# Linear attention into an MLP: k and q loaded ahead of v, and the output step of two head pairs done at once

## The chip, the cores and the metric

The kernel runs on one core of one Trainium2 chip. Its time is the device time of one execution in microseconds (us); the times quoted are medians of several executions. Lower is better. A core has TensorE (PE in the profile, with its weight loads as PEld), VectorE (DVE), ScalarE (ACT), GpSimd (POOL) and SyncE (SP), which work side by side, each through its own instructions in order, and wait for each other on semaphores.

## The reference

Attention with a decay, in blocks of 64 positions, for 4 batches, 8 heads, 768 positions and 64 columns a head; then an MLP with 512 inputs, 2048 hidden columns and 512 outputs over all 3072 tokens.

```python
for b in range(nb):                                   # blocks of 64 positions, in order
    qb, kb, vb = q[:, :, sl], k[:, :, sl], v[:, :, sl]
    intra = einsum('bhic,bhjc->bhij', qb, kb) * Dmask     # lam ** (i - j) for i >= j, else 0
    intra = einsum('bhij,bhjd->bhid', intra, vb)
    inter = einsum('bhid,bhde->bhie', qb * lam_pow, kv_state)
    out[:, :, sl] = intra + inter
    kv_state = lam_block * kv_state + einsum('bhsd,bhse->bhde', kb * rev_pow, vb)
x = out.transpose(0, 2, 1, 3).reshape(B * S, H * D)
h = x @ w_in
return (h / (1 + exp(-1.702 * h))) @ w_out
```

The kernel's own block is 128 positions long; the result is the same.

## The kernel before

**Waves.** The 3072 tokens are done in six waves of 512. Waves 2 to 5 each take 128 positions of all four batches. Waves 0 and 1, on which the change bears, take the first 256 positions of two batches each (`load_big`, `big_cast`, `big_t`, `big_s`, `big_m`, `big_kv`, `big_c`, `big_st`). The eight heads are four pairs, p = 0 to 3; one pair fills the 128 partitions.

**One pair of waves 0 and 1** goes through these steps:

- `load_big` loads k, q or v of some heads, as two DMAs, one for each batch (L96).
- `big_cast` multiplies k and q by powers of lam and casts them to bf16 (L225), on DVE (`V`) or GpSimd (`G_`); `big_cast_v` casts v on GpSimd (L229).
- `big_t` transposes k and q on PE (L238) and copies them out of PSUM, k on ACT (L242), q on ACT or DVE (L240).
- `big_s` makes the scores (L255) and `big_m` masks them on DVE (L262) into `sm` buffers, of which the pool holds six (L261); a pair takes two.
- `big_kv` makes the state of two pairs (L279), in two PSUM banks, one for each half of the 256 positions. ACT copies the first half's state into `mid`, which the second half's output needs (L283, two copies, one for each head), and once more into `first` (L284).
- `big_st` combines the two halves' states on DVE for wave 2 (L291), reading the second half from PSUM.
- `big_c` makes the output of one pair: two full-array matmuls with `mid` (L299) and sixteen on quarter arrays with v and the masked scores (L307), into two banks, which one engine (ACT; DVE for pair 3) casts to `xT` (L311), the MLP's input.

**PSUM.** `bank` hands out eight banks in two rings: three with the tag `mm` (MLP, some transposes) and five with the tag `att`. A step that takes the next bank of its ring waits until its last reader is done.

**MLP.** `mlp1` makes a hidden column block (fc, sixteen of them) from four input blocks kc = 0 to 3, one for each pair (L378), and ACT applies the gelu (L381); `mlp2` makes an output of 128 tokens in four items j (L391). In waves 0 and 1 the first three column blocks (`EARLY = 3`) are started in parts, as the pairs come in: [0, 1], then [2], then [3].

**Order.** The kernel writes each engine's order out by hand (`manual_schedule`); nothing is moved later. The head, wave 0's attention, stands in the main body as a list of calls. Then `main` lists the MLP items wave by wave, and `side` holds calls with the index of the main item ahead of which they are made. `BIG` is that list for wave 1's attention, which so lies among wave 0's `mlp2` items. Matmuls called `fill` multiply zeros while PE has nothing to do.

**Loads.** SP's queue takes the loads of wave 0 in the order q and k of pairs 0 and 1, then v of heads 0 to 3, k, q and v of heads 4 to 7; one DMA that waits for the second block of w_out (`sync_behind_weights`, L188); then wave 1 in the order k, q, v of heads 0 to 3 and k, q, v of heads 4 to 7; then wave 2. Weights come through GpSimd's queue (L176, L180), between its casts. Waves 2 to 5 are cast by `do_cast` and transposed by DMAs on SP's queue (L205).

Of the kernel before, what the change touches and what calls it, by code (L numbers as in the profile page):

```python
# [24 lines left out]
def kernel(  # L25
# [78 lines left out]
    def begin():  # L104
# [8 lines left out]
        for nm, h0 in (("v", 0), ("k", 4), ("q", 4), ("v", 4)):  # L113
            load_big(0, nm, h0, 4, nc.sync)
# [50 lines left out]
    first_sb = [const.tile([P, 2, BB, D], bf16, name=f"first{i}") for i in range(2)]  # L165
# [25 lines left out]
    cast, trans, masked, xT, g_of, h_ps, o_ps, vbig, sc_of, kv_of = ({} for _ in range(10))  # L191
# [27 lines left out]
    def big_cast(w, nm, p, eng):  # L219
# [4 lines left out]
        for bb in range(BB):  # L224
            eng.tensor_tensor(x[:, bb].rearrange("p t (h d) -> p h t d", h=2), pair_of(w, nm, p)[:, bb], by, op=MUL)  # L225
# [6 lines left out]
    def big_t(w, p, q_out=None, mm=None):  # L232
        kq = work.tile([P, 2, BB, 2, P], bf16, tag=f"kq{p}", name="kqB")
        for i, nm in enumerate("kq"):
# [4 lines left out]
            if nm == "q" and q_out is not None:  # L239
                q_out.tensor_copy(kq[:, i], ps_t)  # L240
            else:
                nc.scalar.copy(kq[:, i], ps_t)  # L242
        trans[w, p] = kq
# [24 lines left out]
    def big_kv(w, p0, mm, fills=0):  # L268
# [12 lines left out]
        for h in range(2):  # L281
            hs = slice(64 * h, 64 * h + 64)
            nc.scalar.copy(mid_sb[p0 // 2][hs, :, :, hs], ps_kv[0][hs])  # L283
        nc.scalar.copy(first_sb[p0 // 2], ps_kv[0])  # L284
        kv_of[w, p0] = ps_kv[1]

    def big_st(w, p0):
        ps_kv = kv_of.pop((w, p0))
# [5 lines left out]
    def big_c(w, p, fills=0, x_out=None):  # L294
        vb, qT = vbig[w, p], trans[w, p][:, 1]
        ps_o = [bank([P, BB, 2, D], f32, f"ps_o{r}") for r in range(2)]
        fill(ps_o[0].rearrange("p b t s -> p (b t s)"), fills)
        for bb in range(BB):
            nc.tensor.matmul(ps_o[1][:, bb], mid_sb[p // 2][:, p % 2, bb, :], qT[:, bb, :, D:P],  # L299
                             start=(bb == 0), stop=False, skip_group_check=True)  # L300
        for bb in range(BB):
            for t in range(2):
# [239 lines left out]
```

## Time and profile before

| | us |
|---|---|
| median of three executions | 215.24 |
| lowest, highest | 214.95, 216.2 |
| profiled execution | 215.14 |
| its span, first to last instruction | 213.4 |
| PE busy | 204.8 |
| ACT, DVE, POOL busy | 87.4, 83.8, 33.2 |

The page's second part cuts the span into 40 slices, one digit each, the busy share in tenths. The groups give line, engine, operation, shapes and count, then the busy time in us, the mean length in ns, the idle time ahead of them and what ended it. A line of the timeline has start and busy time in us, then the same names, and in brackets the idle time ahead and its releaser. A busy time of PE includes about 0.2 us in which the last matmul runs out, while the next may have begun.

### The profile page before, as it was taken

To read this page: it belongs to the slowest core of one execution; us is meant where nothing else is said; L and a number is where in the kernel's file an instruction comes from. 1 tells how busy PE (TensorE), PEld (TensorE's weight loads), DVE (VectorE), ACT (ScalarE), POOL (GpSimd) and SP (SyncE) were. 2 spreads that over 40 slices of the span, in tenths; PEclk is the share of its full clock that TensorE was granted. 3 is DMA by queue.
4 is the path that set the end of the run, shared out by engine and by line. 5 is a ranking of instruction groups with operands and counts; after the bars stand their busy time and mean duration, and the time that the engine had idled before them with its cause. 6 is when DMAs were issued, how large, how long until landed. Compare 5 with 4: busy or idle time off the path is not lost.

```text
span 213.4 us, 4323 instructions
## 1 busy us (share of the span) xinstructions
PE 204.8 (96%) x1757; PEld 101.1 (47%) x1757; DVE 83.8 (39%) x186; ACT 87.4 (41%) x164; POOL 33.2 (16%) x62
## 2 busy tenths in 40 slices
PE   7779999999999999999999999999999999999994
PEld 2454444545444455444545444545444545444453
DVE  3687100285751573624272624272624071100121
ACT  4683673445666122366302366302376302466000
POOL 4599000562130012101110001120000000000000
PEclk9999999999999999999999999999999999999999
DMA  5999999999899989699981399981390012100112
GB/s 137 268 248 198 203 197 248 295 267 200 186 276 213 198 190 229 221 188 223 221 195 52 114 184 223 227 191 56 114 178 0 3 51 94 53 2 0 49 49 98
DMA packets 88839, 33.83 MB, mean 159 GB/s; under 512 B 68724, under 2 KB 85876, under 8 KB 88820
## 3 DMA queue, kind: packets, MB, share of 16 engines
q1 hardware_dynamic: 83524, 29.11, 57.9%
q0 software_dynamic: 4752, 4.19, 12.5%
q10 hardware_dynamic: 544, 0.26, 0.5%
q8 instruction: 13, 0.21, 0.4%
q14 instruction: 6, 0.05, 0.1%
HBM read 27.27 MB, written 6.29 MB: 157 GB/s over the span
## 4 chain that ended last, share of the span: by engine, by line
PE 91%; DMA 4%; DVE 1%; ACT 1%; POOL 1%; SPq 0%; issue 0%; POOLq 0%
PE ps_h L378 39%; PE ps_out L391 38%; DMA vb<-in_v_dram 2%; PE ps_o L362 2%; PE ps_o L355 2%; PE ps_s L321 2%; PE ps_part L402 2%; DMA qb<-in_q_dram 2%; PE ps_o L307 1%; PE ps_s L255 1%; PE ps_kv L279 1%; PE ps_kv L338 1%; ACT xT L311 1%; PE ps_tq L238 1%; ACT g_sb L381 1%; POOL vb L229 1%
## 5 line engine op out<-in xcount | busy, mean ns | idle before, releaser
L378 PE MATMUL ps_h<-xT,w_in 128*128 128x512 bf16 x384 | 85.3, 379 | 1.1 <-ACT xT L311 0.5
L391 PE MATMUL ps_out<-w_out,g_sb 128*128 128x512 bf16 x368 | 83.7, 379 | 0.0
L381 ACT ACTIVATE g_sb<-ps_h 128x512 bf16<-128x512 f32 x96 | 56.9, 597 | 44.9 <-PE ps_h L378 44.6
L378 PEld LDWEIGHTS <-w_in 128*128 128x128 bf16 x384 | 37.0, 98 | 45.5 <-issue 1.6
L391 PEld LDWEIGHTS <-g_sb 128*128 128x128 bf16 x368 | 34.5, 98 | 40.2
L325 DVE SCALAR_TENSOR_TENSOR sm<-ps_s,inv_pow,mask 128x512 bf16<-128x512 f32 x32 | 21.8, 744 | 28.6 <-PE ps_s L321 28.6
L395 DVE COPY o_sb<-ps_out 128x512 f32<-128x512 f32 x19 | 13.1, 691 | 47.0 <-PE ps_out L391 46.6
L367 ACT CAST xT<-ps_o 128x512 bf16<-128x512 f32 x16 | 8.6, 589 | 44.4 <-PE ps_o L362 44.4
L202 POOL CAST v_sb<-vf 128x512 bf16<-128x512 f32 x16 | 10.4, 652 | 84.8 <-DMA vf<-in_v_dram 84.8
L225 DVE TENSOR_TENSOR kqb<-kb,kb_pow 128x256 bf16<-128x256 f32 x14 | 6.3, 492 | 19.7 <-DMA kb<-in_k_dram 17.1
L262 DVE SCALAR_TENSOR_TENSOR smb<-ps_s,inv_pow,mask_b 128x512 bf16<-128x512 f32 x16 | 11.0, 745 | 5.9 <-PE ps_s L255 4.8
L345 DVE SCALAR_TENSOR_TENSOR kv<-kv,blk_pow,ps_kv 128x256 bf16<-128x256 bf16 x12 | 5.2, 478 | 17.2 <-PE ps_kv L338 17.2
L200 DVE TENSOR_SCALAR kqs<-qf,q_pow 128x256 bf16<-128x256 f32 x32 | 11.1, 348 | 0.6 <-DMA qf<-in_q_dram 0.6
L225 POOL TENSOR_TENSOR kqb<-qb,qb_pow 128x256 bf16<-128x256 f32 x12 | 7.8, 663 | 22.0 <-DMA qb<-in_q_dram 19.7
L199 DVE TENSOR_SCALAR kqs<-kf,k_pow 128x256 bf16<-128x256 f32 x32 | 11.1, 347 | 0.0
L395 ACT COPY o_sb<-ps_out 128x512 f32<-128x512 f32 x4 | 2.3, 585 | 10.4 <-PE ps_out L391 10.4
L242 ACT COPY kqB<-ps_tk 128x512 bf16<-128x512 bf16 x8 | 4.6, 594 | 2.5 <-PE ps_tk L238 2.4
L238 PEld LDWEIGHTS <-kqb 128*128 128x128 bf16 x64 | 3.9, 98 | 3.6 <-DVE kqb L225 1.3
L355 PEld LDWEIGHTS <-kv 64*64 64x64 bf16 x128 | 3.8, 106 | 3.4 <-issue 3.4
L217 PE MATMUL fill<-warm 128*128 128x512 bf16 x10 | 4.0, 584 | 1.3 <-DVE i_blk L135 1.3
L321 PEld LDWEIGHTS <-kqT 64*128 64x128 bf16 x128 | 3.6, 94 | 3.4 <-issue 3.4
L229 POOL CAST vb<-vb 128x512 bf16<-128x512 f32 x8 | 4.7, 616 | 3.3 <-DMA vb<-in_v_dram 3.2
(61 smaller groups left out, 99.5 us busy)
## 6 DMA issues: line engine op xcount, KB each, us to landing
out_dram<-o_sb SPq DMA_DIRECT2D x23, 256.0 KB, 2.0
kf<-in_k_dram SPq DMA_DIRECT2D x32, 128.0 KB, 3.3
qf<-in_q_dram SPq DMA_DIRECT2D x32, 128.0 KB, 3.5
vf<-in_v_dram SPq DMA_DIRECT2D x32, 128.0 KB, 3.4
vb<-in_v_dram SPq DMA_DIRECT2D x8, 256.0 KB, 5.2
w_out<-in_moe_w_out_dram POOLq DMA_DIRECT2D x4, 512.0 KB, 14.2
kb<-in_k_dram SPq DMA_DIRECT2D x6, 256.0 KB, 5.5
qb<-in_q_dram SPq DMA_DIRECT2D x6, 256.0 KB, 5.9
```

Source lines behind the costliest of these rows:

```text
L199: nc.vector.tensor_scalar(ks[:, :, h, :], kf[:, :, h, :], scalar1=k_pow[:, hd : hd + 1], scalar2=None, op0=MUL)
L200: nc.vector.tensor_scalar(qs[:, :, h, :], qf[:, :, h, :], scalar1=q_pow[:, hd : hd + 1], scalar2=None, op0=MUL)
L202: nc.gpsimd.tensor_copy(v_sb[w % 2][p], vf)
L225: eng.tensor_tensor(x[:, bb].rearrange("p t (h d) -> p h t d", h=2), pair_of(w, nm, p)[:, bb], by, op=MUL)
L262: nc.vector.scalar_tensor_tensor(sm.rearrange("p b t s -> p b (t s)"), s2.rearrange("p b t s -> p b (t s)"), inv_pow[:, 2 * p + h : 2 * p ...
L325: nc.vector.scalar_tensor_tensor(sm, s2[p, h], inv_pow[:, 2 * p + h : 2 * p + h + 1], mask.to_broadcast([P, B, P]), op0=MUL, op1=MUL)
L355: nc.tensor.matmul(ps_o[p][hs, b, :], kv_sb[w % 2][p][hs, b, :], trans[w, p][hs, 1, b, :], start=(b == 0), stop=False, skip_group_check=True)
L367: nc.scalar.copy(x, ps_o[p].rearrange("p b s -> p (b s)"))
L378: nc.tensor.matmul(h_ps[fc], w_in_sb[j][:, kc, i * P : (i + 1) * P], xT[w, kc], start=(kc == 0), stop=(kc == KC - 1))
L381: nc.scalar.activation(g_of[w][:, fc, :], h_ps.pop(fc), GELU)
L391: nc.tensor.matmul(ps_out, g_of[w][:, fc, g * P : (g + 1) * P], w_out_sb[j][:, fc % CW, :], start=(fc == 0), stop=(fc == FFC - 1))
L395: (nc.scalar.copy if w == 0 else nc.vector.tensor_copy)(o, ps_out)
```

## The change

- Loads: in wave 0 v of heads 0 to 3 goes behind k and q of heads 4 to 7; in wave 1 all k and q go ahead of all v.
- Order of the head: transposes and scores of all four pairs are made before the states; then state of pairs 0 and 1, output of pairs 0 and 1, state of pairs 2 and 3, output of pairs 2 and 3; then the MLP, whose early parts are now [0, 1] and [2, 3]. In `BIG` wave 1 is ordered in the same way.
- `big_c` does two pairs in one call: four mid matmuls, thirty-two quarter ones, two banks that each hold both pairs; ACT casts one bank, DVE the other. `xT` is one tile for two pairs (`x_tile`), in all waves.
- `big_kv` copies both halves' states to SBUF as f32 (`part_sb`, on ACT), where `first_sb` held one in bf16; for pairs 2 and 3 one of the two mid copies is on DVE. `big_st` combines the states on GpSimd, two operations a pair, where DVE did one.
- Some casts change engine, the fills are set anew, and some weight loads are called later.

```diff
-        for nm, h0 in (("v", 0), ("k", 4), ("q", 4), ("v", 4)):
+        for nm, h0 in (("k", 4), ("q", 4), ("v", 0), ("v", 4)):
...
-        for h in range(2):
+        for h, eng in enumerate(engs):
             hs = slice(64 * h, 64 * h + 64)
-            nc.scalar.copy(mid_sb[p0 // 2][hs, :, :, hs], ps_kv[0][hs])
-        nc.scalar.copy(first_sb[p0 // 2], ps_kv[0])
-        kv_of[w, p0] = ps_kv[1]
+            eng(mid_sb[p0 // 2][hs, :, :, hs], ps_kv[0][hs])
+        for r in range(2):
+            nc.scalar.copy(part_sb[p0 // 2][r], ps_kv[r])
...
     def big_st(w, p0):
-            nc.vector.scalar_tensor_tensor(kv_sb[0][p][:, BB * w : BB * w + BB], first_sb[p0 // 2][:, i],
-                                           blk_pow[:, p : p + 1], ps_kv[:, i], op0=MUL, op1=ADD)
+            nc.gpsimd.tensor_scalar(part_sb[p0 // 2][0][:, i], part_sb[p0 // 2][0][:, i], scalar1=blk_pow[:, p : p + 1],
+                                    scalar2=None, op0=MUL)
+            nc.gpsimd.tensor_tensor(kv_sb[0][p][:, BB * w : BB * w + BB], part_sb[p0 // 2][0][:, i],
+                                    part_sb[p0 // 2][1][:, i], op=ADD)
...
+    def big_c(w, p0, fills=0):
+        ps_o = [bank([P, 2, BB, 2, D], f32, f"ps_o{r}") for r in range(2)]
...
+        x = x_tile(w, p0)
+        for r, eng in enumerate((nc.scalar.copy, nc.vector.tensor_copy)):
+            eng(x.rearrange("p i (b r s t) -> p r (i b) t s", b=BB, r=2, t=2)[:, r],
+                ps_o[r].rearrange("p i b t s -> p (i b) t s"))
+
+    def x_tile(w, p0):
+        x = xp.tile([P, 2, W], bf16, tag=f"x{p0}", name="xT")
+        for i in range(2):
+            xT[w, p0 + i] = x[:, i]
+        return x
...
-    BIG = [(27, big_cast, "k", 0, V), (27, big_cast, "q", 0, G_), (27, big_cast, "k", 1, V), (27, big_cast, "q", 1, G_),
-           (27, big_cast_v, 0), (27, big_cast_v, 1), (30, big_t, 0), (31, big_t, 1), (31, big_s, 0), (31, big_m, 0),
-           (32, big_s, 1), (32, big_m, 1), (32, big_cast, "k", 3, G_), (32, big_cast, "k", 2, V),
-           (34, big_kv, 0, False), (34, big_cast, "q", 2, G_), (34, big_cast, "q", 3, V), (34, big_st, 0),
-           (35, big_c, 0), (35, big_c, 1), (35.5, big_t, 2, V, True), (36, big_t, 3, V),
-           (36.5, big_s, 2), (36.5, big_m, 2), (37, big_s, 3), (37, big_m, 3), (37, big_cast_v, 2), (37, big_cast_v, 3),
-           (38, big_kv, 2, False), (41, big_c, 2), (41, big_c, 3, 0, V.tensor_copy), (41, big_st, 2)]
+    AV = (nc.scalar.copy, V.tensor_copy)
+    BIG = [(24, big_cast, "k", 0, V), (24, big_cast, "q", 0, G_), (24, big_cast, "k", 1, V), (24, big_cast, "q", 1, G_),
+           (24, big_cast, "k", 2, G_), (27, big_t, 0), (28, big_t, 1), (28, big_s, 0), (28, big_m, 0),
+           (29, big_cast, "k", 3, V), (29, big_s, 1), (29, big_m, 1),
+           (29, big_cast, "q", 2, G_), (29, big_cast, "q", 3, V),
+           (31, big_t, 2, "kq", AV, True), (31, big_t, 3, "kq", AV), (31, big_cast_v, 0), (31, big_cast_v, 1),
+           (32, big_s, 2), (32, big_m, 2), (32, big_s, 3), (32, big_m, 3),
+           (33, big_kv, 0, False), (33, big_cast_v, 2), (33, big_cast_v, 3), (34, big_c, 0), (34, big_kv, 2, False, 0, AV),
+           (35, big_c, 2), (36, big_st, 0), (36, big_st, 2)]
...
-        return ([(mlp1, w, fc, kcs) for kcs in ([0, 1], [2], [3]) for fc in range(EARLY)]
+        return ([(mlp1, w, fc, kcs) for kcs in ([0, 1], [2, 3]) for fc in range(EARLY)]
...
+        big_cast(0, "k", 2, G_)
+        load_w_in(0)
+        load_w_in(1)
+        f1 = bank([P, W], f32, "fill", True)
+        fill(f1, 6)
+        big_cast(0, "k", 3, V)
+        big_cast(0, "q", 2, V)
+        big_cast(0, "q", 3, V)
+        big_t(0, 2, "k")
+        big_t(0, 3, "k")
+        big_t(0, 2, "q")
+        big_t(0, 3, "q")
         big_cast_v(0, 0)
         big_cast_v(0, 1)
...
+        big_s(0, 2)
+        big_m(0, 2)
+        big_s(0, 3)
+        big_m(0, 3)
+        big_kv(0, 0, True)
+        big_c(0, 0, 2)
...
+        big_kv(0, 2, False, 2, AV)
+        big_c(0, 2)
         late_mask()
+        big_st(0, 0)
+        big_st(0, 2)
         sync_behind_weights()
         big_tiles(1)
-        for g in range(2):
-            for nm in "kqv":
-                load_big(1, nm, 4 * g, 4, nc.sync)
+        for nm, h0 in (("k", 0), ("q", 0), ("k", 4), ("q", 4), ("v", 0), ("v", 4)):
+            load_big(1, nm, h0, 4, nc.sync)
```

Because the early items are six where they were nine, an index in the new `BIG` stands for the same place as one three higher in the old.

More of the change, by code (lines that the diff above doesn't have):

```diff
@@ L164 @@
     kv_sb = [[const.tile([P, B, D], bf16, name=f"kv{i}{p}") for p in range(NP)] for i in range(2)]
-    first_sb = [const.tile([P, 2, BB, D], bf16, name=f"first{i}") for i in range(2)]
+    part_sb = [[const.tile([P, 2, BB, D], f32, name=f"part{i}{r}") for r in range(2)] for i in range(2)]
     mid_sb = [const.tile([P, 2, BB, P], bf16, name=f"mid{i}") for i in range(2)]
@@ L364, in mix @@
         ps_kv = state_mm(w, pairs)
-        for p in pairs:
-            x = xp.tile([P, W], bf16, tag=f"x{p}", name="xT")
-            nc.scalar.copy(x, ps_o[p].rearrange("p b s -> p (b s)"))
-            xT[w, p] = x
+        x = x_tile(w, pairs[0])
+        for i, p in enumerate(pairs):
+            nc.scalar.copy(x[:, i], ps_o[p].rearrange("p b s -> p (b s)"))
         state_up(w, pairs, ps_kv)
```

83 lines of the change are left out of this document (30 added, 53 removed).

## The prediction

> **What bounds the kernel now.** I read the page first: its busy times, its slices, and the groups that give the prices of single operations (the last row is of the groups of PE in the first 60 us).
>
> ```profile
> PE 204.8 (96%) x1757; PEld 101.1 (47%) x1757; DVE 83.8 (39%) x186; ACT 87.4 (41%) x164; POOL 33.2 (16%) x62
> PE   7779999999999999999999999999999999999994
> PEclk9999999999999999999999999999999999999999
> L395 DVE COPY o_sb<-ps_out 128x512 f32<-128x512 f32 x19 | 13.1, 691 | 47.0 <-PE ps_out L391 46.6
> L367 ACT CAST xT<-ps_o 128x512 bf16<-128x512 f32 x16 | 8.6, 589 | 44.4 <-PE ps_o L362 44.4
> L262 DVE SCALAR_TENSOR_TENSOR smb<-ps_s,inv_pow,mask_b 128x512 bf16<-128x512 f32 x16 | 11.0, 745 | 5.9 <-PE ps_s L255 4.8
> L299 PE MATMUL ps_o<-kqB,mid 128*128 128x128 bf16 x16 | 2.3, 223 | 0.0
> ```
>
> PE is the bound: only the first slices (5.3 us each) are not full. So the change can act in two places: before the MLP of wave 0 has its inputs, and where wave 1's attention is woven into wave 0's output matmuls. Behind that all code is the same but for the layout of xT. Next, PE in order of time (start, busy, what, idle before).
>
> ```profile
> 20.96 1.46 PE L378 MATMUL ps_h<-xT,w_in 128*128 128x512 bf16 x6 [0.27 <-ACT xT L311]
> 22.67 11.38 PE L378 MATMUL ps_h<-xT,w_in 128*128 128x512 bf16 x52 [0.25 <-ACT g_sb L381]
> 33.90 7.07 PE L391 MATMUL ps_out<-w_out,g_sb 128*128 128x512 bf16 x32
> 40.80 0.39 PE L238 MATMUL ps_tk<-ident,kqb 128*128 128x128 bf16 x4
> ...
> 46.20 0.45 PE L279 MATMUL ps_kv<-vb,kqb 64*64 64x64 bf16 x32
> 46.58 1.04 PE L391 MATMUL ps_out<-w_out,g_sb 128*128 128x512 bf16 x4
> 47.60 0.29 PE L299 MATMUL ps_o<-kqB,mid 128*128 128x128 bf16 x2
> ...
> 48.17 0.28 PE L299 MATMUL ps_o<-kqB,mid 128*128 128x128 bf16 x2
> 48.38 0.42 PE L307 MATMUL ps_o<-smb,vb 64*64 64x128 bf16 x16
> 48.73 1.04 PE L391 MATMUL ps_out<-w_out,g_sb 128*128 128x512 bf16 x4
> ...
> 55.45 0.42 PE L307 MATMUL ps_o<-smb,vb 64*64 64x128 bf16 x16
> 56.15 1.46 PE L378 MATMUL ps_h<-xT,w_in 128*128 128x512 bf16 x6 [0.27 <-ACT xT L311]
> 57.85 10.52 PE L378 MATMUL ps_h<-xT,w_in 128*128 128x512 bf16 x48 [0.25 <-ACT g_sb L381]
> ```
>
> From 22.67 to 33.90 are 52 matmuls, 0.216 us each. Twelve of the 64 ran before, so wave 0's MLP stands as if it had begun at 22.67 - 12 x 0.216 = 20.08 without a gap. That is the head's figure to beat. In wave 1 time is lost in three places: 47.60 - (46.58 + 4 x 0.216) = 0.16 for the mid copies, (56.15 - 55.45) - (48.73 - 48.38) = 0.35 for xT, and 57.85 - (56.15 + 6 x 0.216) = 0.41 for the first gelu.
>
> **The head, part by part.** When loads land is read where an idle engine was released by them. These are POOL, DVE, ACT in their order of time.
>
> ```profile
> 10.34 1.17 POOL L229 CAST vb<-vb 128x512 bf16<-128x512 f32 x2 [2.10 <-DMA vb<-in_v_dram]
> 13.96 0.61 POOL L225 TENSOR_TENSOR kqb<-qb,qb_pow 128x256 bf16<-128x256 f32 x1 [0.19 <-DMA qb<-in_q_dram]
> 16.05 1.18 POOL L229 CAST vb<-vb 128x512 bf16<-128x512 f32 x2
> 12.17 1.10 DVE L225 TENSOR_TENSOR kqb<-kb,kb_pow 128x256 bf16<-128x256 f32 x3 [0.39 <-DMA kb<-in_k_dram]
> 13.19 1.67 DVE L225 TENSOR_TENSOR kqb<-qb,qb_pow 128x256 bf16<-128x256 f32 x2
> 20.73 0.78 DVE L311 CAST xT<-ps_o 128x256 bf16<-128x256 f32 x2 [1.03 <-PE ps_o L307]
> 11.91 0.76 ACT L283 CAST mid<-ps_kv 64x256 bf16<-64x256 f32 x2
> ```
>
> *Loads.* The four-head transfers end at about 10.3 (v 0), 12.2 (k 4) and 13.9 (q 4); v 4 follows one step later, about 15.7. Same bytes, same queue, so the slots stay and the contents change: k 4 at 10.3, q 4 at 12.2, v 0 at 13.9, v 4 at 15.7. GpSimd takes the cast of k of pair 2 when it lands, then issues two weight loads, then the casts of v: k's two casts stand where v's two stood, so the weights come about when they did.
>
> *k, q, scores.* DVE's casts for pairs 2 and 3 (six left to it, at a step of about 0.34 from the 12.17 row) run from 11.3 to 13.4; transposes, copies and all scores are done before 15. They are hidden behind v: v 0's casts take 13.9 to 15.1 (1.17), and now they are done at 11.5. This is the price of the reordering.
>
> *The serial tail.* State matmuls of pairs 0 and 1 end at 15.5 (half of 0.45 behind the last cast); two ACT mid copies 0.76, so 16.3; the double output step for pairs 0 and 1 from 16.35. It costs 0.85: two single steps now take 48.73 - 47.60 = 1.13. In one of them 48.38 - 48.17 = 0.21 pass from the first mid matmul to the first quarter-array one, where two mid matmuls need a step of 0.07 each (0.29 busy, 0.22 for one); the 0.14 left is a switch of the array, and joining drops two. The last mask of pair 3 now waits: `sm` has six buffers (L261), pairs 0 to 2 hold all six, and the first is freed when the double step has read pair 0: 0.35 to its first quarter matmul, 0.2 for sixteen, 0.22 for the last to end, so at 17.1. In the order before, pair 0's output step had long run by then. So on DVE: two masks, 0.66 apart, start 17.1, DVE free at 18.45; then its half of xT; then its half of the second mid copy. A DVE cast of 128x512 from PSUM has no row; it lies between 0.69 (the f32 copy, L395) and 0.78 (two casts of 128x256); I take 0.69, as size and source are the same, of which 0.60 before the next may start. The mid half lies between 0.37 (ACT's 0.76 for two) and 0.44 (half of 0.78 and the overlap); I take 0.44, DVE's own. That gives 19.1 and 19.5. The second double step starts at 19.55, and the MLP, 0.9 with the switch, at 20.45. Behind it nothing waits: its xT needs 0.69 and the six matmuls ahead of [2, 3] give 1.29; the first gelu, 0.6, lies under the rest. 20.45 against 20.08: **+0.37**. The copies of both states into f32 and GpSimd's combination run beside it; were they not hidden, ACT's two copies would add about 0.6.
>
> **Wave 1.** DVE, POOL and SP there:
>
> ```profile
> 43.17 2.73 DVE L262 SCALAR_TENSOR_TENSOR smb<-ps_s,inv_pow,mask_b 128x512 bf16<-128x512 f32 x4 [3.34 <-PE ps_s L255]
> 40.51 1.75 POOL L225 TENSOR_TENSOR kqb<-qb,qb_pow 128x256 bf16<-128x256 f32 x3 [0.21 <-DMA qb<-in_q_dram]
> 45.92 0.78 POOL L225 TENSOR_TENSOR kqb<-qb,qb_pow 128x256 bf16<-128x256 f32 x1 [0.28 <-DMA qb<-in_q_dram]
> 47.83 1.17 POOL L229 CAST vb<-vb 128x512 bf16<-128x512 f32 x2 [1.13 <-DMA vb<-in_v_dram]
> 62.73 6.21 SPq L205 DMA_TRANSPOSE kqT<-kqs  x4
> ```
>
> Here too the slots stay: v 0 takes the slot that ended at 45.9, v 4 that of 47.8. All PE times shift by the 0.37.
>
> - *q of pair 3.* DVE now does masks of pair 0 (from 43.54, two steps of 0.66), k of pair 3 (0.68), masks of pair 1 (1.32): q of pair 3 starts at 46.85. Until 47.06 GpSimd casts v 0, and DVE's cast waits for it: where both ran, two DVE casts took 1.67 (13.19 row), 0.84 each, against 0.37 for one of three (12.17 row). It ends at 47.7. PE comes to their second half at about 47.25: the output matmuls ahead end where the state matmuls start now (46.20, less the switch, plus 0.37 is 46.5), and fourteen transposes at 0.055 follow (four in 0.39, 0.22 of it one alone). **+0.50**.
> - *The second state step.* Of five PSUM banks its second is that of pair 3's scores, whose masks wait again for the double output step. From the start c of that step: masks from c + 0.77, bank free at c + 1.55; PE wants it at c + 0.8: **+0.75**.
> - *The second mid copy.* Two masks (1.32), xT (0.60), mid (0.44) on DVE end at c + 3.15; PE is there at c + 0.8 + 0.75 + 0.4 for the state matmuls + 0.9 for four output ones = c + 2.85: **+0.33** with the release.
> - *Gone:* 0.10 of the 0.16 of the mid wait, 0.35 and 0.41 at the MLP (xT of pairs 0 and 1 is older, and [2, 3] in one gives the gelu 0.43 more), and two switches in each of the two double steps, 0.57: **-1.43**.
>
> Sum of wave 1: 0.50 + 0.75 + 0.33 - 1.43 = +0.15. Whole change: +0.52. The profiled execution took 215.14 (span 213.4 and 1.74 around it), 0.10 under the median 215.24; so 215.66 beside it, and as a median 215.76, **215.8**.
>
> [...]
>
> **Rivals.**
> *Faster: the mask ring does not bind and the loads come earlier.* Then the second double step follows its state step, wave 0's MLP begins near 19.2, and wave 1 has +0.50 - 1.43. Against it: code and rows give the wait, and PE cannot use the head's gain. The first transposes of wave 1 need q 0, cast at 40.51 + 0.61 = 41.1, when PE is there now (40.80 plus 0.3); and the scores of wave 2 need the second transpose issued behind 62.73 (PE's row, and the transposes' own view):
>
> ```profile
> 68.31 0.62 PE L321 MATMUL ps_s<-kqT 64*128 64x128 bf16 x16
> DMA to landing us min/median/max: 3.2/3.5/4.6
> ```
>
> issued about 1.8 after the first (a quarter of 6.21, the first ones slower) and 3.5 in flight, it lands near 68.1, and PE's second half of that group starts at 68.55. With the ring free but the loads where they are, 214.9; only with both 214.1. Chance 0.07.
>
> *No net loss: v 0 lands 0.4 sooner, or DVE's pieces are shorter by as much.* The head's +0.37 vanishes, wave 1 keeps +0.15: 215.2 to 215.4. Chance 0.14.
>
> *Slower: DVE and GpSimd collide in wave 1.* If the head is late by 0.8 more, as when v 0 lands at 14.7 because weight loads got between, q of pair 3 is cast from 47.6 and falls on v 4's casts (47.83, 1.17): two halves that wait, 1.67 for 0.74, +0.9. In all 215.24 + 0.52 + 0.8 + 0.9 = 217.5. It decides from 0.8 late on. Chance 0.15.
>
> *Slower: the clock falls.* PE idles for 1.2 before the second double step (its state matmuls end near 18.3), and of the 19 fills that follow the first ten only 15 stay.
>
> ```profile
> 1.25 4.02 PE L217 MATMUL fill<-warm 128*128 128x512 bf16 x10 [1.25 <-DVE i_blk L135]
> 15.76 0.38 PE L238 MATMUL ps_tq<-ident,kqb 128*128 128x128 bf16 x4 [0.62 <-DVE kqB L240]
> ```
>
> These first ones took 0.40 each, not 0.216: a cold stretch of 4 us costs 1.9, so 217.7. A gap of 0.62 in the head left the granted clock full. [...] Chance 0.07.
>
> *A strided DVE cast dearer than 0.78* (1.2, say, at two places): 216.5. Chance 0.07.
>
> **The numbers.** The forecast itself, 215.4 to 216.2, has 0.50. What a measurement here can tell from no change is about 0.5%, 1.08 us: 214.16 to 216.32. Faster 0.07; same 0.50 + 0.14 = 0.64; slower 0.15 + 0.07 + 0.07 = 0.29. The range, 214.8 to 217.5, leaves out the fastest and the clock, 0.14.
>
> **What would show it.** Right: in the head DVE's masks of pair 3 idle until PE's output step releases them near 17.1; PE waits before the second double step for a DVE mid copy; the MLP of wave 0 starts near 20.4 and runs without its two gaps; in wave 1 PE waits for q of pair 3 near 47.5, and for a mask before the second state step. Wrong: a wave 0 MLP under 20 or over 21, a wave 1 without a wait on a mask, halved matmuls after 18, or scores of wave 2 that wait for their transposes.

## The result: slower by 0.84%

The changed kernel takes 217.62 us (median of 18 executions, 216.53 to 218.52), the kernel before beside it 215.69 (18 executions, 214.5 to 217.51). The ratio is 1.0084, with a 95% interval of 1.006 to 1.0107. Forecast were 215.8 us and a range of 214.8 to 217.5, with "same" as the likeliest; it is slower, and just outside the range. The profiled execution took 217.62 with a span of 215.8, where the kernel before had 215.14 and 213.4.

Counting the runs below, the changed kernel was executed 32 times; the kernel before ran 110 times beside these added runs. One execution of the kernel before and three of the versions below were in a slower state and are left out of the ratios. The median spans are 215.7 and 213.5, so the span grew by 2.2, where +0.52 was forecast. Spans are used below beside the times, because the time outside the span differs from kernel to kernel (last section).

### The profile page after: what moved, and what is told of

It reads as the page before. It is cut to its first block, busy times and chain, and to the rows that moved or that the text cites. A ratio compares the mean times of both kernels' runs of the same rounds, so it can differ in the third digit from the quotient of the medians.

```text
span 215.8 us, 4315 instructions
## 1 busy us (share of the span) xinstructions
PE 207.1 (96%) x1753; PEld 101.4 (47%) x1753; DVE 83.3 (39%) x179; ACT 87.7 (41%) x160; POOL 40.9 (19%) x77
## 4 chain that ended last, share of the span: by engine, by line
PE 89%; DVE 5%; DMA 2%; issue 1%; ACT 1%; SPq 0%; DVEq 0%
PE ps_h L385 39%; PE ps_out L398 36%; DVE smb L260 2%; PE ps_o L370 2%; PE ps_o L363 2%; PE ps_s L329 2%; DMA kb<-in_k_dram 2%; DVE kqb L225 2%; PE ps_part L409 2%; PE ps_s L253 1%; PE ps_o L308 1%; ACT kqB L241 1%; PE ps_o L298 1%; PE ps_kv L346 1%; PE ps_tq L240 1%
## 5 line engine op out<-in xcount | busy, mean ns | idle before, releaser
L385 PE MATMUL ps_h<-xT,w_in 128*128 128x512 bf16 x384 | 86.3, 385 | 0.0
L225 DVE TENSOR_TENSOR kqb<-kb,kb_pow 128x256 bf16<-128x256 f32 x12 | 5.1, 463 | 20.7 <-DMA kb<-in_k_dram 18.1
L200 DVE TENSOR_SCALAR kqs<-qf,q_pow 128x256 bf16<-128x256 f32 x32 | 11.8, 368 | 0.0
L199 DVE TENSOR_SCALAR kqs<-kf,k_pow 128x256 bf16<-128x256 f32 x32 | 11.8, 368 | 0.0
L225 POOL TENSOR_TENSOR kqb<-qb,qb_pow 128x256 bf16<-128x256 f32 x9 | 5.8, 657 | 17.6 <-DMA qb<-in_q_dram 15.4
L217 PE MATMUL fill<-warm 128*128 128x512 bf16 x16 | 5.9, 538 | 1.2 <-DVE i_blk L135 1.2
L288 POOL TENSOR_SCALAR part<-part,blk_pow 128x128 f32<-128x128 f32 x8 | 4.9, 616 | 4.7 <-ACT part L283 4.7
```

The source lines that it names most:

```text
L199: nc.vector.tensor_scalar(ks[:, :, h, :], kf[:, :, h, :], scalar1=k_pow[:, hd : hd + 1], scalar2=None, op0=MUL)
L200: nc.vector.tensor_scalar(qs[:, :, h, :], qf[:, :, h, :], scalar1=q_pow[:, hd : hd + 1], scalar2=None, op0=MUL)
L385: nc.tensor.matmul(h_ps[fc], w_in_sb[j][:, kc, i * P : (i + 1) * P], xT[w, kc], start=(kc == 0), stop=(kc == KC - 1))
```

## The profile after

The same rows of the page of the changed kernel:

```profile
PE 207.1 (96%) x1753; PEld 101.4 (47%) x1753; DVE 83.3 (39%) x179; ACT 87.7 (41%) x160; POOL 40.9 (19%) x77
PE   7887999999899999999999999999999999999994
PEclk9999799999999999999999999999999999999999
```

PE is busy 2.3 us longer than the 204.8 of before with four matmuls fewer, and its granted clock has a dent in the fifth slice that the kernel before has not. PE of the changed kernel in order of time (start, busy, what, idle before):

```profile
17.78 0.44 PE L277 MATMUL ps_kv<-vb,kqb 64*64 64x64 bf16 x30 [0.15 <-DVE smb L260]
19.53 0.40 PE L298 MATMUL ps_o<-kqB,mid 128*128 128x128 bf16 x4 [1.32 <-DVE mid L281]
...
20.43 15.67 PE L385 MATMUL ps_h<-xT,w_in 128*128 128x512 bf16 x64
35.94 7.07 PE L398 MATMUL ps_out<-w_out,g_sb 128*128 128x512 bf16 x32
42.85 0.39 PE L240 MATMUL ps_tk<-ident,kqb 128*128 128x128 bf16 x4
...
48.10 0.39 PE L240 MATMUL ps_tk<-ident,kqb 128*128 128x128 bf16 x4
...
49.41 1.03 PE L398 MATMUL ps_out<-w_out,g_sb 128*128 128x512 bf16 x4
...
54.10 0.22 PE L277 MATMUL ps_kv<-vb,kqb 64*64 64x64 bf16 x2
54.91 0.44 PE L277 MATMUL ps_kv<-vb,kqb 64*64 64x64 bf16 x30 [0.60 <-DVE smb L260]
...
56.67 0.40 PE L298 MATMUL ps_o<-kqB,mid 128*128 128x128 bf16 x4 [0.35 <-DVE mid L281]
...
57.57 13.12 PE L385 MATMUL ps_h<-xT,w_in 128*128 128x512 bf16 x60
70.63 0.62 PE L329 MATMUL ps_s<-kqT 64*128 64x128 bf16 x16
```

The head came as forecast, to the hundredths: the second double output step waits for DVE's mid copy until 19.53 (19.55), and the MLP of wave 0 begins at 20.43 (20.45). But its 64 matmuls take until 35.94, 15.51 us, where 64 x 0.216 are 13.8. Wave 1's first transposes so start at 42.85, 2.05 later than the 40.80 of before; its MLP, at 57.57, stands 2.31 later than before's effective start (57.85 - 12 x 0.216 = 55.26); the last output is 2.3 later. So wave 0 lost 2.05 and wave 1 only 0.26. Windows of 3.41 us of the same execution (window, its length, PE busy, granted clock, DMA share, GB/s), and below them one of the kernel before:

```profile
13.73:17.14 3.41, 2.85 (x105) 1.00 1.30 184
17.14:20.55 3.41, 1.94 (x75) 1.00 1.22 166
20.55:23.96 3.41, 3.41 (x9) 0.50 1.17 189
```

```profile
8.12:11.53 3.41, 2.08 (x45) 1.00 0.96 273
```

The clock is at half for one stretch of 3.41 us (20.55 to 23.96), which begins just as the MLP does (20.43). Nine matmuls ran in it. Ahead of it lies a window in which PE was busy for 1.94 us and never idle for more than 1.32 at a stretch. In the profile of the kernel before the emptiest window of that length up to the MLP, wherever it begins, had 2.04 us (2.08 in the row above), and the clock held. It does not always hold there: in 6 of the 110 executions the mean granted clock was 0.99 too, and these took 216.5 (median) where all took 215.4. The rival "the clock falls" had named this, with the place and a price of 1.9, and had been given 0.07.

## The experiments

**Is it the clock? The change again, five times.** The mean granted clock of an execution tells whether it had the stretch: 0.99 with it (3.41 of 215.8 us at half are 0.008 of the mean), 1.00 without.

> The changed kernel unchanged, for a second profile beside its times and clocks. Theory 'clock': the slowdown is the half-clock stretch of 3.4 us that begins where the MLP of wave 0 does (64 matmuls in 15.67 instead of 13.9 us). An execution whose mean granted clock reads 1.00 has no such stretch and should then take about 215.9, one at 0.99 about 217.6. Rival 'order': the time is in the order of the work (the head's chain of waits on DVE, wave 1's waits), and the clock costs little: executions at 1.00 and at 0.99 take the same, 217.5 both, and a profile without the stretch shows another wait of 1.5 us or more.

Measured: 217.35, ratio 1.0084 [1.0055, 1.0112]. Taken with the other executions of the changed kernel, 21 of 32 had the stretch. Those take 217.6 (median), the 11 others 217.2. So the clock alone does not explain the result: without the stretch the kernel is still 1.8 slower than the 215.4 of before. To see what those lose, a profile without the stretch was needed; the first four all had it.

> The changed kernel unchanged, for one more profile. About one execution in three has had a mean granted clock of 1.00, and those took 217.2 on average against 217.7 for those at 0.99. Theory 'two covers': in a profile at 1.00 the MLP of wave 0 is 1.7 sooner (first output copy of wave 0 at 40.4 instead of 42.2), and PE then waits 0.8 to 1.3 for the q of wave 1's pair 0, which lands after 40.7, so that the span is shorter by 0.3 to 0.8 only. Rival: the time is lost elsewhere, behind 60 us. A profile at 0.99 repeats the one there is: 217.6.

> The same once more: at a clock of 1.00 a wait of PE for wave 1's first q of 0.8 to 1.3 and a span of 215.0 to 215.5; at 0.99 a half-clock stretch, no such wait, and a span of 215.5 to 216.5.

> The changed kernel unchanged, for a profile without the half-clock stretch, which its four profiles so far all have. At a clock of 1.00: first output copy of wave 0 at 40.4 to 40.9, a wait of PE for wave 1's first q of 0 to 1.3, and wave 1's waits for q of pair 3, the mask ring and the second mid copy as in the others. At 0.99: 217.5 or 218.2, as q of pair 3 is cast beside GpSimd's cast of v or not.

Measured: 217.54, 218.25 and 216.90, with spans of 215.7, 216.4 and 214.9. The last had no stretch; its PE:

```profile
20.28 13.99 PE L385 MATMUL ps_h<-xT,w_in 128*128 128x512 bf16 x64
34.10 7.07 PE L398 MATMUL ps_out<-w_out,g_sb 128*128 128x512 bf16 x32
41.01 0.39 PE L240 MATMUL ps_tk<-ident,kqb 128*128 128x128 bf16 x4
...
46.45 0.39 PE L240 MATMUL ps_tk<-ident,kqb 128*128 128x128 bf16 x4
...
48.09 0.62 PE L240 MATMUL ps_tq<-ident,kqb 128*128 128x128 bf16 x4 [0.81 <-DVE kqb L225]
48.55 1.03 PE L398 MATMUL ps_out<-w_out,g_sb 128*128 128x512 bf16 x4
...
56.72 3.63 PE L385 MATMUL ps_h<-xT,w_in 128*128 128x512 bf16 x16
```

The MLP of wave 0 takes 34.10 - 20.28 = 13.82, so the stretch costs 15.51 - 13.82 = 1.69, and without it the head is late by 0.21 (41.01). But wave 1 now loses 1.25 (56.72 - 55.26 = 1.46 at its MLP) instead of 0.26. Most of it stands between 46.45 and 48.55: sixteen transposes and the wait for q of pair 3 take 2.10, where before they took 50.50 - 49.61 = 0.89. That is a wait of 1.21. The same subtraction gives 49.41 - 48.10 - 0.89 = 0.42 in the profile above, and 0.45, 1.21 and 1.24 in the three others with a stretch. The two rows of the kernel before:

```profile
49.61 0.39 PE L238 MATMUL ps_tk<-ident,kqb 128*128 128x128 bf16 x4
...
50.50 1.03 PE L391 MATMUL ps_out<-w_out,g_sb 128*128 128x512 bf16 x4
```

DVE and POOL of the execution without the stretch, then of the first profile:

```profile
44.83 1.19 DVE L225 TENSOR_TENSOR kqb<-kb,kb_pow 128x256 bf16<-128x256 f32 x2
45.94 1.40 DVE L260 SCALAR_TENSOR_TENSOR smb<-ps_s,inv_pow,mask_b 128x512 bf16<-128x512 f32 x2
47.26 1.11 DVE L225 TENSOR_TENSOR kqb<-qb,qb_pow 128x256 bf16<-128x256 f32 x2
...
44.79 0.61 POOL L225 TENSOR_TENSOR kqb<-qb,qb_pow 128x256 bf16<-128x256 f32 x1 [0.28 <-DMA qb<-in_q_dram]
46.60 1.17 POOL L229 CAST vb<-vb 128x512 bf16<-128x512 f32 x2 [1.20 <-DMA vb<-in_v_dram]
```

```profile
46.49 0.75 DVE L225 TENSOR_TENSOR kqb<-kb,kb_pow 128x256 bf16<-128x256 f32 x2
48.48 0.75 DVE L225 TENSOR_TENSOR kqb<-qb,qb_pow 128x256 bf16<-128x256 f32 x2
...
47.11 1.17 POOL L229 CAST vb<-vb 128x512 bf16<-128x512 f32 x2 [1.20 <-DMA vb<-in_v_dram]
48.86 1.40 POOL L229 CAST vb<-vb 128x512 bf16<-128x512 f32 x2 [0.58 <-DMA vb<-in_v_dram]
```

The two casts of k take 1.19 where they meet a GpSimd cast of q, and those of q 1.11 where they meet its cast of v; each takes 0.75 in the other profile, where it begins ahead of GpSimd's cast. GpSimd's start is set by the loads here (1.20 us idle for a load ahead of the first cast of v in both), DVE's by PE (3.32 and 4.62 idle behind the scores, ahead of the masks from 43.51 and 45.16). A PE that comes 1.7 sooner while the loads come when they come meets them. So the stretch is partly paid back: it moves DVE's casts out of the way of GpSimd's. It need not do so, as two profiles with a stretch and a wait of 1.2 show (218.28 and 218.25 us).

**The clock kept up: filling matmuls.**

```diff
-        big_c(0, 2)
+        big_c(0, 2, 5)
```

> Five filling matmuls of 128x512 ahead of the second double output step of wave 0, in the 1.3 us in which PE waits for DVE's mid copy (18.2 to 19.5). They take 5 x 0.216 = 1.08 us and fit. Theory 'clock': the clock stays full, the 64 matmuls of the MLP of wave 0 take 13.8 to 13.9 instead of 15.67, all later times come 1.7 sooner: 215.9, ratio to the kernel before 1.001. Rival 'order': the MLP starts at 20.43 as before and everything behind takes as long: 217.5, ratio 1.008.

Measured: 217.69, ratio 1.0104 [1.0061, 1.0147]. None of the six executions had the stretch, and the MLP of wave 0 began at 20.3. The span fell only to 215.2. In its profile PE waits 1.2 us for wave 1's first q, cast late because its load was late (0.5 and 0.4 us of idle time behind GpSimd's cast):

```profile
41.87 0.29 PE L240 MATMUL ps_tq<-ident,kqb 128*128 128x128 bf16 x2 [0.48 <-POOL kqb L225]
42.55 0.28 PE L240 MATMUL ps_tq<-ident,kqb 128*128 128x128 bf16 x2 [0.40 <-POOL kqb L225]
```

So both theories failed: no execution had the fall of the clock, and that brings 0.5 of the 1.7. The filling matmuls make the fall rarer, not impossible: with the same five, two of six executions with early loads and two of six with early weights (both below) had it.

**One half of the change at a time.** First the new head alone: wave 1 with the loads, the list and the steps of before (`old_`).

```diff
-           (33, big_kv, 0, False), (33, big_cast_v, 2), (33, big_cast_v, 3), (34, big_c, 0), (34, big_kv, 2, False, 0, AV),
-           (35, big_c, 2), (36, big_st, 0), (36, big_st, 2)]
+           (31, old_kv, 0, False), (31, big_cast, "q", 2, G_), (31, big_cast, "q", 3, V), (31, old_st, 0),
+           (32, old_c, 0), (32, old_c, 1), (32.5, old_t, 2, V, True), (33, old_t, 3, V),
...
+           (35, old_kv, 2, False), (38, old_c, 2), (38, old_c, 3, 0, V.tensor_copy), (38, old_st, 2)]
```

> The new order in wave 0's head alone: wave 1 has the loads, the order, the single output steps, the copies and the state step on DVE of the kernel before. Theory 'clock': head +0.37 and the stretch +1.7, of which wave 1's loads give nothing back: 217.3, ratio 1.0075 to 1.01. Rival 'wave 1': what costs is wave 1's order; the head is worth no more than 0.4: 215.6 to 216.0, ratio 1.000 to 1.002.

Then the new order in wave 1 alone.

```diff
-        for nm, h0 in (("k", 4), ("q", 4), ("v", 0), ("v", 4)):
+        for nm, h0 in (("v", 0), ("k", 4), ("q", 4), ("v", 4)):
...
-        big_kv(0, 0, True)
-        big_c(0, 0, 2)
+        old_kv(0, 0, False, 3)
+        big_cast(0, "k", 2, V)
+        old_c(0, 0, 8)
+        old_c(0, 1)
```

> The new order in wave 1 alone: wave 0's head has the loads, the order, the fills, the single output steps and the copies of the kernel before. Theory 'clock': no stretch; wave 1's waits (q of pair 3, the second state step's bank, the second mid copy) against its gains: +0.2 to +0.6 us, 215.9 to 216.3, ratio 1.001 to 1.003. Rival 'wave 1': the whole loss is here, 217.5, ratio 1.008.

Measured: 216.77, ratio 1.0052 [1.0026, 1.0077], for the head alone; 216.56, ratio 1.0048 [1.0021, 1.0075], for wave 1 alone. The median spans are 215.0 and 214.4, so +1.5 and +0.9, together 2.4, near the 2.2 of the whole change. The head was forecast at +0.37 and wave 1 at +0.15: both forecasts were too low, and neither rival ("all in one half") holds. In the first, 9 of 11 executions had the stretch; in the second none of 12. In the profile of the first it began at 14.72, ahead of the MLP, whose matmuls then ran at full clock (20.95 to 34.55); that execution took only 215.73.

**Wave 1's loads sooner.** They were started behind another block of weights, without and with the filling matmuls.

```diff
-        nc.sync.dma_start(out=behind, in_=w_out_sb[1][0:1, 0, 0:2])
+        nc.sync.dma_start(out=behind, in_=w_out_sb[0][0:1, 0, 0:2])
```

> The changed kernel with wave 1's loads started behind the first block of w_out instead of the second, some 2.5 us sooner (the two landed at 29.90 and 32.48 in the changed kernel's profile). Theory 'two covers': the slow clock of the head (1.7 us) and PE's wait for wave 1's first q (1.2 us in the profile with filling matmuls) lie over each other, so that taking one away alone gives little. Here the wait is taken away and the clock is not: executions with the half-clock stretch stay at 217.6, those without come to 216.4, median 217.0 to 217.5, ratio 1.006 to 1.009. Rival 'loads': wave 1's loads are the whole cost, 216.3 in all executions, ratio 1.003. Rival 'order': the waits on DVE and on the mask ring are all of it, 217.5, in all executions.

> Both taken away: wave 1's loads behind the first block of w_out, and five filling matmuls ahead of the second double output step. Theory 'two covers': 217.7 less 1.2, 216.4, ratio 1.004, PE's first transposes of wave 1 without a wait, a head at +0.2 and a wave 1 at +0.5 against the kernel before. Rival 'order': 217.6. Rival 'contention': the loads now fall on the last blocks of w_out, and the output matmuls of wave 0 wait for these near 37.7: no gain, and the wait is seen there.

Measured: 217.51, ratio 1.0107 [1.007, 1.0145], and 217.91, ratio 1.0121 [1.0091, 1.0151]. The edit missed its aim. The second half of q of pair 0 was cast from 41.9 (with the filling matmuls; from 40.5 in the kernel before). That the sooner loads shared the DMA engines with the last blocks of w_out is an explanation that was not shown. The rival "contention" was right that there is no gain. But the wait for w_out that it named is hardly there (the 32 output matmuls took 0.1 longer); PE still waits for wave 1's first q, 0.21 and 0.40.

**The mask ring.** The last edit, and eight buffers, in both places that use the ring (the second serves waves 2 to 5):

```diff
-            sm = work.tile([P, BB, 2, P], bf16, tag="sm", bufs=6, name="smb")
+            sm = work.tile([P, BB, 2, P], bf16, tag="sm", bufs=8, name="smb")
...
-                sm = work.tile([P, B, P], bf16, tag="sm", bufs=6, name="sm")
+                sm = work.tile([P, B, P], bf16, tag="sm", bufs=8, name="sm")
```

> As the one before, and eight buffers for the masks instead of six. Theory: the masks of pair 3 no longer wait for the double output step, in the head (MLP of wave 0 0.5 sooner) and in wave 1 (no wait of 0.75 before the second state step, none of 0.35 for the second mid copy, but DVE's q of pair 3 is still late): 0.8 to 1.1 less in all, 215.5, ratio 1.000. Rival: the ring does not matter, since the second state step then waits for a bank or for v: 216.4, ratio 1.004.

Measured: 216.96, ratio 1.0076 [1.0051, 1.0102]: 0.95 less than without it, and 1.25 less in the median span. PE's wait before the second state step (0.60) is gone from the profile, that for the second mid copy falls from 0.35 to 0.26. The head gained nothing, since its filling matmuls themselves came late (three of them behind 0.60 of idle time, below).

**q of pair 3 on GpSimd**, on top of that:

```diff
-           (29, big_cast, "q", 2, G_), (29, big_cast, "q", 3, V),
+           (29, big_cast, "q", 2, G_), (29, big_cast, "q", 3, G_),
```

> As the one before, and in wave 1 q of pair 3 scaled on GpSimd instead of DVE, where it stands behind the masks of pair 1. Theory: PE no longer waits before the last four transposes (0.5 to 1.2 in the profiles so far): 0.5 to 1.0 less, 214.6 to 215.0, ratio 0.995 to 0.998, the first version faster than the kernel before. Rival: GpSimd's casts of v come 1.2 later for it and PE waits for these at the first state step: 215.5, ratio 1.000.

Measured: 216.22, ratio 1.0029 [1.0001, 1.0057]: 0.74 less again, with no wait left in the last transposes, and GpSimd's later casts of v cost nothing (the first state step, at 50.89, waits for nothing). But the median span falls by 0.15 only (214.5 to 214.35). In its profile wave 1's MLP begins 0.9 sooner (55.62 for 56.54), and then the scores of wave 2 wait 0.80 for their transposes: most of the 0.74 lies outside the span.

**The weights' place in GpSimd's queue.** In the change two blocks of w_in are issued between and behind the casts of v. DMA rates from 19 to 21 us (window, length, granted clock, DMA share, GB/s) of the kernel before, the changed kernel and the next experiment:

```profile
19.00:20.00 1.00, 1.00 1.25 205
20.00:21.00 1.00, 1.00 1.22 204
```

```profile
19.00:20.00 1.00, 1.00 1.31 171
20.00:21.00 1.00, 0.78 1.04 136
```

```profile
19.00:20.00 1.00, 1.00 1.20 199
20.00:21.00 1.00, 1.00 1.28 213
```

```diff
         load_w_in(1)
+        load_w_in(2)
+        load_w_in(3)
...
-        load_w_in(2)
...
-        for j in range(3, len(IN_COLS)):
-            load_w_in(j)
+        load_w_in(4)
```

> The changed kernel with the third and fourth block of w_in issued by GpSimd right behind the second, ahead of the casts of v, where the changed kernel issues them between and behind these. Theory 'late weights': in the change the weight queue runs dry near 19 to 20 us (114 to 147 KB per us there in the runs so far, 200 to 207 before and after), so that wave 1's loads, which start behind the weights, land 0.3 to 1.4 later than in the kernel before, and without the half-clock stretch PE waits for the first q. With the blocks issued early the second block of w_out lands at 31.2 to 31.8 and wave 1's q of pair 0 by 40.3; span less by 0.3 to 0.5 in executions with the stretch, by 1.0 to 1.2 without: median 216.9, ratio 1.005. Rival 'order': only the waits on DVE count, 217.5.

> As the one before, and five filling matmuls ahead of the second double output step. Theory 'two covers' with 'late weights': now both are gone, the head is at +0.2 to +0.4 against the kernel before and wave 1 at +0.3: span 214.0 to 214.2, 215.9, ratio 1.002 to 1.003. Rival 'order': 217.6 as with the filling matmuls alone. If q of pair 0 still lands after 41, the lateness is not of the weights, and the time stays at 217.6.

> The kernel before with nothing changed but the place of one weight load: GpSimd issues the fourth block of w_in behind its casts of the last v, as the change does, and no longer ahead of them. Theory 'late weights': the queue runs dry near 19, the later blocks and wave 1's loads land 0.4 to 0.9 later, PE waits for the first q and for the transposes of wave 2: 215.9 to 216.4, ratio 1.002 to 1.004. Rival 'order': no change, 215.4, ratio 1.000.

Measured: 217.24, ratio 1.0084 [1.0058, 1.0111]; with the filling matmuls 217.75, ratio 1.0103 [1.0063, 1.0143]; and the kernel before with one block issued late 216.01, ratio 1.0014 [0.9984, 1.0044], which tells nothing from no change. The gap in the DMA rate is filled, and the second half of wave 1's q of pair 0 is cast from 39.5 and 40.3 (40.5 in the kernel before, 40.0 in that kernel with the late block, 41.2 in the changed one), but little time comes of it. In the profile without the filling matmuls the stretch began at 14.80; in the one with them PE stood still for 1.18 without a releaser (below). In both the wait for q of pair 3 was long, 1.0 and 1.1; in the second the earlier loads brought GpSimd's first casts of v (1.36) under DVE's casts of k (1.43).

**Clock and weights mended, by filling matmuls at another place.**

```diff
-        big_kv(0, 2, False, 2, AV)
+        big_kv(0, 2, False, 6, AV)
```

> The early weight blocks once more, and the clock kept up by other means: four more filling matmuls of 128x256 (4 x 0.109 = 0.44 us) ahead of the second state step of wave 0, where PE waits for the last mask and DVE's chain sets the end, instead of five of 128x512 behind it, where PE ran out of instructions in two runs. Theory 'two covers': clock and first q both gone, head +0.4, wave 1 +0.3 to +0.9 (q of pair 3): 216.0 to 216.7, ratio 1.002 to 1.005, against 1.0084 with the weights alone. Rival 'clock counts little': 217.2 as with the weights alone. Rival 'instructions': the fetch of PE's next block of instructions, which began between 16.1 and 17.6 in the runs so far, ends after 19.5 here too, and the head is late by 0.5 to 1.0 whatever the clock: 217.2 to 217.7, and the wait stands at the output step.

Measured: 217.18, ratio 1.0076 [1.0049, 1.0102]. "Two covers" fell: four of the five executions compared had no stretch and took as long; the rival "clock counts little" had the time. In the profile the first q was early (second half cast from 39.2), and the wait for q of pair 3 (1.24) and the mask ring were still there.

**Only the two waits mended**: eight mask buffers and q of pair 3 on GpSimd, nothing else.

> The changed kernel with eight mask buffers and q of pair 3 of wave 1 scaled on GpSimd, and nothing else: no filling matmuls, the weight blocks where the change has them. Theory 'waits': of the 1.9 us that the change costs, the mask ring (0.95 by e8 against e7) and q of pair 3 (0.74 by e9 against e8) are 1.7, so 215.7 to 215.9, ratio 1.000 to 1.001, and the clock and the late loads matter little. Theory 'clock and loads': wave 0's MLP is late by 0 to 2 by the stretch, and wave 1's loads by 0 to 1, so that the scores of wave 2 come no sooner: 216.2 to 216.6, ratio 1.003 to 1.005, against 0.998 for e12, which had both mended.

Measured: 215.93, ratio 1.0021 [0.9996, 1.0046], span 214.05. Two edits take back 1.6 of the 2.2 in the span. The stretch came in 4 of 12 executions, and these were no slower (215.6 against 216.0). Its PE:

```profile
18.76 0.40 PE L298 MATMUL ps_o<-kqB,mid 128*128 128x128 bf16 x4 [0.93 <-DVE mid L281]
...
19.66 4.71 PE L385 MATMUL ps_h<-xT,w_in 128*128 128x512 bf16 x21
...
41.45 0.29 PE L240 MATMUL ps_tq<-ident,kqb 128*128 128x128 bf16 x2 [0.67 <-POOL kqb L225]
42.28 0.28 PE L240 MATMUL ps_tq<-ident,kqb 128*128 128x128 bf16 x2 [0.55 <-POOL kqb L225]
```

With the ring free the second double step comes 0.8 sooner (18.76 for 19.53), the MLP at 19.66, 0.4 before the kernel before. Then PE waits 1.2 for wave 1's first q: what the head gains, the loads take. Against the profile without the stretch (216.90) wave 1's MLP begins 1.38 sooner (55.34 for 56.72): 0.62 come from the head, 1.21, 0.77 and 0.09 from the three waits of wave 1, and the first q takes 1.38 back. Theory "waits" so gave the size, but as the rest of a larger gain, and with a price for q that was hardly in the span (above); "clock and loads" is right about what bounds next.

**All of it, and the other way about.** First all the mends together (early weights, three filling matmuls, eight buffers, q on GpSimd); then the old head with the new wave 1, eight buffers and q on GpSimd.

> As the one before (three filling matmuls), with eight mask buffers and, in wave 1, q of pair 3 scaled on GpSimd. Theory: head at -0.1, wave 1 without its waits at -1.2 against the kernel before, until the scores of wave 2, which wait for the transposes behind wave 1's loads; with these loads no later than in the kernel before, span 212.6 to 213.4, 214.4 to 215.2, ratio 0.995 to 0.999. Rival 'loads bind': wave 1's loads land as late as in the runs so far, the scores of wave 2 wait, and the span stays at 214.4, 216.2, ratio 1.003.

> The kernel before in wave 0's head, the change in wave 1, with eight mask buffers and q of pair 3 scaled on GpSimd: the waits that the change brought are gone from wave 1, and its gains (one double step less its switches, no wait for xT and the first gelu) remain. Theory: wave 1's MLP 0.9 to 1.2 sooner than in the kernel before, until the scores of wave 2 wait for their transposes, which lie behind wave 1's loads: span 0 to 0.5 less, 214.9 to 215.5, ratio 0.997 to 1.000. Rival: GpSimd's later casts of v hold up the first state step: 215.9, ratio 1.002.

Measured: 215.13, ratio 0.998 [0.9951, 1.001], and 215.14, ratio 0.9982 [0.9956, 1.0008], with a median span of 213.2 in both, 0.3 under the kernel before. They are the best versions found, and cannot be told from it. The first lies in its forecast, but not by the way that was expected: its head was to gain 0.1, and in its profile the MLP of wave 0 begins at 21.19, 1.1 late (last section). The second begins wave 1's MLP 0.4 sooner than the kernel before, and then its scores of wave 2 wait:

```profile
68.07 0.40 PE L381 MATMUL ps_s<-kqT 64*128 64x128 bf16 x8
69.31 0.40 PE L381 MATMUL ps_s<-kqT 64*128 64x128 bf16 x8 [0.85 <-DMA kqT<-kqs]
```

## Why the prediction was wrong, point by point

The terms in the first profile and in the one without the stretch. The second state step is 54.91 - 54.10 (54.06 - 53.24 in the other) less one step of 0.05; the mid copy is the idle time of its row. (The forecast's 0.41 for the first gelu is 0.40 by its own rows.)

| term, us | forecast | with the stretch | without (216.90) |
|---|---|---|---|
| head, up to the MLP | +0.37 | +0.35 | +0.20 |
| half clock in wave 0's MLP | 0 | +1.69 | 0 |
| wave 1's first q | 0 | 0 | +0.13 |
| q of pair 3 | +0.50 | +0.42 | +1.21 |
| second state step | +0.75 | +0.76 | +0.77 |
| second mid copy | +0.33 | +0.35 | +0.35 |
| what is gone (the remainder) | -1.43 | -1.26 | -1.20 |
| sum at wave 1's MLP | +0.52 | +2.31 | +1.46 |

- **The forecast rested on a full clock**, and that step failed. The sum put the half clock at 0, and it cost 1.69 in the first profile. The rival had the fall, the place, the 15 filling matmuls that stay of 19, and the price (1.9 for 1.69). Its chance, 0.07, leaned on a gap of 0.62 that had left the clock full; that a gap of 1.2 would do the same was the author's estimate, which no run had shown. A single gap also says little of a stretch in which PE is busy for 1.94 of 3.41 us; 21 of 32 executions had the fall. But this is not the whole miss: without the stretch the time is still 217.2 (median), 1.4 above the forecast.
- **q of pair 3 was sized without its neighbour.** The step started it at 46.85, from a k of pair 3 that takes 0.68, and let only q meet GpSimd. In the execution without the stretch k meets GpSimd too (1.19), q starts at 47.26 and meets the cast of v (1.11). The term measured 1.21 for 0.50, which is 0.71 of the 0.94 by which that execution's sum exceeds the forecast. That the two engines hold each other up was right, near the size that the 1.67 of before had given (DVE's two casts took 1.19 and 1.11 for 0.75, GpSimd's two beside them in the first profile 1.40 for 1.17). The rival "DVE and GpSimd collide" had the mechanism at another pair of casts (q of pair 3 on the later v); it ended at 217.5 and had 0.15.
- **Right:** the head's chain by the mask ring, what the double step saves (0.84 from 53.26 to 54.10, for 0.85; that switches of the array are the reason was not tried), the mask that holds up the second state step (0.76 for 0.75) and the second mid copy, and that GpSimd's combination is off the path. That the head agrees to the hundredths is luck: the masks were released 0.13 sooner (16.97 for 17.1), and DVE's half of xT took 0.75 for 0.60. Wave 2's casts take longer beside GpSimd's work, by 1.5 in all (58.36 to 61.41 for six that alone need 0.26 each), and at no cost (the scores of wave 2, at 70.63, wait for nothing). Most of it is beside GpSimd's casts of wave 2's v (59.43 to 61.34), which come behind the combination; beside the combination itself the first two casts take 0.45 and 0.37. DVE of the changed kernel, the first row beside the casts of v, the second behind them:

```profile
60.17 0.69 DVE L199 TENSOR_SCALAR kqs<-kf,k_pow 128x256 bf16<-128x256 f32 x1
61.41 0.34 DVE L199 TENSOR_SCALAR kqs<-kf,k_pow 128x256 bf16<-128x256 f32 x1
```

  Taking ring and q away gave back 1.65 in the span, where their three terms sum to 1.58 (0.50 + 0.75 + 0.33), though not term by term (see that run). The floor under wave 2 is there too: 0.85 in the last profile.
- **A smaller miss:** "the weights come about when they did". The DMA rate dips to 136 GB/s and wave 1's first q is cast 0.3 to 1.1 later (40.85, 41.22 and, with the two waits mended, 41.61 for 40.51). It costs nothing while PE is late itself (no wait for that q in the first profile), and becomes the bound once PE is not (1.2 of waiting with the two waits mended).
- **"Slower" had 0.29**, and the likeliest case was "same". A sum of seven terms between -1.43 and +0.75 that ends at +0.52 left little room for one of them.

What stays open: why the executions without the stretch are only 0.4 faster in the median. One profile of them shows a long wait for q of pair 3; whether they all have it was not seen, and at 216.90 it is the fourth fastest of the 11. The mean clock also does not tell where a stretch lay: in the four profiles of the changed kernel that have one it began between 19.6 and 20.6, on the MLP or just ahead of it, but in those of the head alone (14.72) and the early weights (14.80) it was over by 18.2, and the MLP ran at full clock (at work by 20.95 and 20.98).

## What to carry to other kernels

Work moved onto an engine that another can hold up takes as long as what it meets lets it (0.75 for two casts alone, up to 1.55 for the same two here), and what it met was set by the loads, not by the order of calls; price it for both alignments. When two delays stand ahead of the same bound, taking one away can show little: cut the change in halves and mend the waits together before a cause is cleared. Where PE's order is loosened, look at how busy PE stays over several us, not at its longest gap alone: here the clock went to half for 3.41 us with no gap over 1.32 ahead of it.

## What the runs showed of the hardware

- **The clock falls though PE was idle for no more than 1.32 us at a stretch.** The stretch in the first profile is 3.41 us long at a granted clock of 0.50; PE was 57% busy in the 3.41 us ahead of it (1.94). Share of busy time alone does not decide: 61% held in the profile of the kernel before (2.08 of 3.41), and in the run with early weights the clock fell behind a window that was 79% busy, most of it with quarter-array and transposing matmuls:

```profile
11.39:14.80 3.41, 2.69 (x65) 1.00 1.25 255
14.80:18.21 3.41, 3.08 (x76) 0.50 1.35 205
```

- **PE stands still and no releaser is seen.** With all mends, a filling matmul that needed nothing started 2.05 behind the one recorded before it (one of the three has no record, which is 0.2 of that); the profile names no releaser. A transfer of the instruction queue lies ahead of it. That it is the cause is the author's inference and was not shown. PE of that run, and its DMA queues from 17 to 19 us:

```profile
17.65 0.39 PE L217 MATMUL ps_o<-warm 128*128 128x512 bf16 x1
20.09 0.38 PE L217 MATMUL ps_o<-warm 128*128 128x512 bf16 x1 [2.05 <-issue]
```

```profile
q0 software_dynamic: 405, 0.40, 121.6%
q8 instruction: 1, 0.02, 3.0%
```

  Of six profiles with filling matmuls at that place, five stop there, for 0.2 to 2.05 us. In the two with the longest stops (1.18 and 2.05) the transfer began between 17 and 18 us, in the four others between 16 and 17. So in these runs the mends moved the head less than they could: the MLP of wave 0 begins at 21.19 with all of them, and at 19.66 with eight buffers and no added filling matmuls. Whether the transfer is late because of the weights, whose queue takes 121.6% in the rows above, was not tried.
- **Time outside the span.** It was 1.7 to 2.0 us in every execution of the kernels with 1753 matmuls, and 1.7 to 3.4 in those with 1756 to 1758, the kernel before (1757) among them. So a few instructions more go with up to 1.5 us more outside the span in some executions; why was not tried.
